# Block means of the first chunk from its own value rows, and their products apart

## The chip, the cores and the metric

The kernel runs on one core of a Trainium2 chip. The metric is the time of one execution on the device, in microseconds (us). Three runs of the kernel before took 574.43, 574.89 and 575.10 us; the median is 574.89.

## The reference

The kernel computes an attention layer and, on its output, two expert layers (MLPs).

```python
# attention: batch 2, 8 heads, 768 positions, 64 wide
k_sum = k.reshape(B, H, nb, block, D).max(axis=3)      # blocks of 32 keys
v_sum = v.reshape(B, H, nb, block, D).mean(axis=3)
scores_l = scale * q @ k^T, kept where |i - j| < 16, else -1e9
scores_s = scale * q @ k_sum^T + log(32)
a = softmax(concat([scores_l, scores_s]))              # 1e-9 added to the sum
x = a @ concat([v, v_sum])
# two expert layers, 512 -> 2048 -> 512, on 1536 tokens
h = x @ w_in;  g = relu(h) ** 2;               x = g @ w_out
h = x @ w_in2; g = 0, (h + 1) ** 2 / 4 or h;   out = g @ w_out2
```

So each query looks at a band of 16 keys to either side and at 24 block keys. Its output is a product of its probabilities with the values of the band and with the 24 block means of the values.

## The kernel before, in words

**Attention.** The queries are cut into six chunks of 256 (three in each batch), and each chunk into four pairs of heads, which makes 24 tiles. The steps of tile i have short names in a plan: S (scores: 16 matmuls, line 629), M (mask, scale and row maximum, VectorE, line 637), E (exponential, ScalarE, line 643), Q, R and N (sum, reciprocal, normalising), T (four transposes on TensorE, line 660), to (copy of the transposed probabilities out of PSUM, line 663), O (product with the values, line 671), oh and ol (the output as a high and a low part). A score tile has 96 columns for the band of 64 queries and 24 for the block keys, so the transposed probabilities have 120 rows.

The value tile of a chunk, `vwt`, holds for each of its four groups of 64 queries the 96 value rows of the band (rows 0 to 95, step vl) and under them the 24 block means (rows 96 to 119). One matmul then contracts all 120 rows. The block means are made on TensorE: step v (line 697) multiplies a tile of 128 value rows by a matrix `vx` that holds 1/32 in the place of each block, and adds up in a PSUM bank. Six such tiles of plain values (loads bl0 and bl1, line 716, into the value tile of chunk 1 and into scratch) make a batch of 24 means. Step vk copies them to `vs` in SBUF (line 706), and step vf spreads them under the value rows by a DMA from SBUF to SBUF (line 614). For chunk 0 two pairs of heads are spread by ScalarE instead (step f, line 701) and the rest by the DMA.

**Experts.** Weights come as raw 64-bit numbers (wl, line 202) and are taken apart by ScalarE, VectorE and GpSimd (dl, dq, dr, ds, dt, da, wh, wo) into a high and a low part. Step H (line 290) is the first product of an expert layer, Y (line 419) the second, with ha, hb, hh and hl between them. The first twelve such units run in between the attention tiles. Later units use products of a Strassen scheme (Pa to Pg, line 322).

**Order.** There is no scheduler. `PLAN` is a list of 2291 steps; `build` calls them one by one, and each engine runs its instructions in that order. A letter behind a number names the engine (a ScalarE, v VectorE, g GpSimd). `warm7` means seven filler matmuls into an unused bank (line 688). All loads are issued from SP in one queue, in the plan's order, and a load waits there until its buffer is free.

Of the kernel before, what the change touches and what calls it, by code (L numbers as in the profile page):

```python
# [66 lines left out]
to5a ol4 M9 wh2a wo3g O5 ha0a Q8 T6 oh5a M10 hb0 N7g H1 to6a hh0a ol5 E9 R8 wo2g km5 T7 S11 ha1a hl0g Q9 dq4 O6 vf2
N8g Y0 oh6a to7a ol6 wl6 dr4 hb1 bl2 dl4 ds4 O7 wl7 R9 dt4 T8 kl7 N9g oh7a dq5 ol7 H3 M11 wh4a da4 E10 km4 H2 dr5 hh1a
Q10 to8a hl1g S12 E11 ds5 T9 R10 M12 N10g Y1 ha2a hb2 ha3v to9a dt5 dl5 O8 wo4v wh5a S13 wl9 da5 Q11 hb3 vl4 km6 T10
dq6 wl8 H4 E12 ql4 wo5g M13 hh2a R11 oh8v H5 E13 hl2g ol8 dr6 hh3v to10a O9 N11v hl3g ha4a S14 Q13 dq7 dl6 dr7 T11 R13  # L70
ds7 hb4 H6 to11a ds6 M14 hh4a hl4g Y2 oh9v ol9 N13g ha6a km7 v6 dt6 O10 v7 ha5v wh6a da6 Q12 S15 hb6 bl3 dl7 v8 vl3
oh10v H7 E14 R12 ql5 dt7 N12v da7 hb5 Y3 ol10 wh7a M15 hh5a hl5g wo6v E15 v9 O11 v10 wo7v dq8 v11 Y4 hh6v ha7v vk5a
hl6g vk6a Q15 hb7 vk7a dr8 vk4a oh11a Y6 vf3 hh7v ds8 hl7g Q14 vf4 ua0v T12 Y7 to12a R14 dt8 N14g yo7a ol11 uf0v S16
dq9 S17 T13 M16 ug0g H8 to13a M17 dl8 E16 T14 wl10 R15 dr9 O13 N15v O12 to14a ha8v ub0v S18 oh13a E17 S19 Q16 uc0g
oh12v T15 dl9 R16 ol12 Y5 M18 to15a yo5a uh0g ol13 H9 Q17 E18 R17 M19 N16g O15 ha9a Q18 O14 E19 S20 N17g oh15v ol15
hb8 S21 Q19 T16 hh8v R19 H10 M20 hl8g to16a hb9 N19g hh9a T17 E20 M21 H11 da8 oh14v to17a ol14 ui0a S23 ha10v R18 ds9
hb10 S22 N18v E21 O17 dt9 O16 uj0v hh10a wl11 T18 da9 oh16a vl5 LW0 wh9a Y8 Q20 to18a ol16 hl9v oh17a hl10g T19 ol17
R20 Y9 M22 to19a uk0g ha11a M23 wh8a O18 E22 Q21 O19 wo9g N20v Y10 oh19a saa2g oh18a Q22 dq10 ol19 E23 wo8g T20 ol18
R21 H16 sab2v hb11 to20a N21v dq11 dr10 ul0v T21 ha16a H17 hh11a sac2v sh5a Q23 hl11g to21a sl5v hb16 dr11 um0a O21
R22 ds11 N22g O20 hh16a ud0a Y11 hl16 dt11 ha17a sad2v hb17 ds10 T22 sh4a R23 dt10 H18 hh17a sl4g wh11a hl17 oh21a  # L80
N23v dl11 dl10 H19 wl13 ue0v yo11a wl12 da10 to22v ha18v Y16 un0v da11 hb18 ha19a ol21 wh10a oh20a wo10v T23 wo11g Y17
# [733 lines left out]
```

## Time and profile before

| | |
|---|---|
| Median of three runs | 574.89 us (574.43 to 575.10) |
| The profiled execution | 576.15 us, of which the span from first to last instruction is 574.2 us |
| TensorE busy | 565.1 us, 98% of the span |
| VectorE, ScalarE, GpSimd busy | 455.6, 375.6 and 244.6 us (79%, 65%, 43%) |
| Granted TensorE clock, mean | 0.997 |
| DMA | 54.15 MB; 326, 333, 299 and 322 GB/s in the first four of 40 slices, some 75 GB/s in most of the later ones |

The page gives the busy time of each engine, the span in 40 slices, and the chain of work that ended last, followed back from the end. A second view cuts the span into stretches and gives for each the busy time of the engines, the granted clock of TensorE and the share of the DMA engines; what a stretch lacks in busy time is idle time. The timeline lists an engine's instructions in order, each with the idle time ahead of it and what ended that.

### The profile page before, as it was taken

What the parts mean: (1) busy time and instruction counts of PE and PEld (TensorE: products, weight loads), DVE (VectorE), ACT (ScalarE), POOL (GpSimd) and SP (SyncE); (2) the same over time, 40 slices, a digit from 0 to 9 for tenths busy, and PEclk for the clock granted to TensorE, in tenths of its full rate; (3) what the DMA queues carried; (4) which work ended last, traced back from release to release, by engine and by line L of the source; (5) the groups of instructions that cost most, each with busy time, mean ns of one, the idle gap of its engine ahead of it and who ended that gap; (6) DMA issues with size and microseconds to landing.
All of it is one profiled execution on the core that took longest, in us unless ns stands there. A gap on an engine that the chain in (4) does not pass through costs nothing.

```text
span 574.2 us, 11097 instructions
## 1 busy us (share of the span) xinstructions
PE 565.1 (98%) x4207; PEld 526.9 (92%) x4207; DVE 455.6 (79%) x1064; ACT 375.6 (65%) x796; POOL 244.6 (43%) x211
## 2 busy tenths in 40 slices
PE   8899999999999999999999999999999999999997
PEld 3599899999999999999999998989998988999886
DVE  5889989889987776668888988969886897756554
ACT  5789689877755554546574887867756877835450
POOL 3466576543544434535348485414443433310000
PEclk9899999999999999999999999999999999999999
DMA  8889613122222222212221102222222222000005
GB/s 326 333 299 322 209 40 94 74 73 76 74 73 74 74 74 74 75 73 75 75 84 63 42 34 74 73 74 73 75 73 72 76 73 75 1 1 0 1 0 220
DMA packets 16528, 54.15 MB, mean 94 GB/s; under 512 B 1724, under 2 KB 2332, under 8 KB 16476
## 3 DMA queue, kind: packets, MB, share of 16 engines
q1 hardware_dynamic: 16476, 53.45, 26.6%
q8 instruction: 33, 0.54, 0.4%
q14 instruction: 19, 0.16, 0.1%
HBM read 49.41 MB, written 3.15 MB: 92 GB/s over the span
## 4 chain that ended last, share of the span: by engine, by line
PE 95%; DMA 3%; ACT 1%; DVE 0%; SPq 0%; issue 0%; ACTq 0%
PE bank L419 45%; PE bank L322 36%; PE bank L290 6%; PE bank L671 2%; PE bank L629 2%; PE bank L660 2%; DMA raw<-in_wd_dram 2%; PE bank L480 1%; DMA q<-in_qd_dram 1%; PE bank L697 0%; ACT fx L213 0%; ACT s L643 0%; SPq L202 0%; ACT acc L706 0%; DVE sm L646 0%
## 5 line engine op out<-in xcount | busy, mean ns | idle before, releaser
L222 POOL TENSOR_TENSOR fr<-fx,fr 128x512 uint32<-128x512 uint32 x64 | 88.9, 1398 | 149.8 <-DVE fx L219 79.1
L386 DVE TENSOR_TENSOR gl<-bank,gh 128x384 fp32r<-128x384 f32 x120 | 65.2, 550 | 14.5 <-ACT gh L382 13.4
L322 PE MATMUL bank<-xl,wih 128*128 128x384 f32 x224 | 75.1, 335 | 0.0
L322 PE MATMUL bank<-xh,wih 128*128 128x384 f32 x224 | 74.9, 334 | 0.0
L419 PE MATMUL bank<-gh,woh 128*128 128x384 f32 (+1 forms) x272 | 64.8, 329 | 0.0
L361 ACT ACTIVATE tm<-bank,bias 128x384 f32<-128x384 f32 x62 | 35.8, 577 | 44.3 <-PE bank L322 23.9
L419 PE MATMUL bank<-gl,woh 128*128 128x384 f32 (+1 forms) x272 | 63.7, 325 | 0.0
L419 PE MATMUL bank<-gh,wol 128*128 128x384 f32 (+1 forms) x272 | 63.7, 325 | 0.0
L378 DVE SCALAR_TENSOR_TENSOR bank<-bank,tm 128x384 f32<-128x384 f32 x64 | 35.5, 561 | 29.9 <-ACT tm L374 28.8
L322 PE MATMUL bank<-xh,wil 128*128 128x384 f32 x224 | 57.0, 335 | 0.0
L322 PE MATMUL bank<-tl,wih 128*128 128x384 f32 x168 | 56.3, 335 | 0.0
L322 PE MATMUL bank<-th,wih 128*128 128x384 f32 x168 | 56.2, 334 | 0.0
L419 PE MATMUL bank<-woh,gl 128*128 128x512 f32 x180 | 55.8, 391 | 0.0
L419 PE MATMUL bank<-wol,gh 128*128 128x512 f32 x180 | 55.8, 391 | 0.0
L419 PE MATMUL bank<-woh,gh 128*128 128x512 f32 x180 | 55.7, 391 | 0.0
L448 DVE TENSOR_TENSOR acc<-bank,acc 128x384 f32<-128x384 f32 (+1 forms) x81 | 46.5, 603 | 6.1 <-PE bank L419 5.8
L213 ACT ACTIVATE fx<-raw 128x512 f32<-128x512 f32 x64 | 42.4, 669 | 8.3 <-DMA raw<-in_wd_dram 5.9
L208 ACT ACTIVATE fr<-raw 128x512 uint32<-128x512 uint32 x64 | 42.3, 671 | 8.3 <-POOL wil L258 3.0
L419 PEld LDWEIGHTS bank<-gh,woh 128*128 128x128 f32 x272 | 47.3, 188 | 0.5 <-issue 0.2
L419 PEld LDWEIGHTS bank<-gh,wol 128*128 128x128 f32 x272 | 47.5, 188 | 0.0
L419 PEld LDWEIGHTS bank<-gl,woh 128*128 128x128 f32 x272 | 47.5, 188 | 0.0
L382 ACT CAST gh<-bank 128x384 fp32r<-128x384 f32 x78 | 36.8, 479 | 15.7 <-DVE bank L378 14.4
(145 smaller groups left out, 1395.4 us busy)
## 6 DMA issues: line engine op xcount, KB each, us to landing
raw<-in_wd_dram SPq DMA_DIRECT2D x64, 512.0 KB, 3.6
vw<-in_vw_dram SPq DMA_DIRECT2D x4, 1024.0 KB, 8.1
k<-in_kd_dram SPq DMA_DIRECT2D x8, 400.0 KB, 5.9
out_dram<-acc SPq DMA_DIRECT2D x11, 256.0 KB, 3.6
q<-in_qd_dram SPq DMA_DIRECT2D x5, 512.0 KB, 8.3
vw<-in_vb_dram SPq DMA_DIRECT2D x1, 1024.0 KB, 8.9
acc<-in_vb_dram SPq DMA_DIRECT2D x2, 512.0 KB, 7.3
acc<-in_vw_dram SPq DMA_DIRECT2D x1, 1024.0 KB
```

The lines of the kernel that those rows point to most:

```text
L208: A.activation(fr[n % 2], w_raw(n, 0), AF.Copy, scale=2.0 ** -29)
L213: A.activation(f32(x), f32(hi), AF.Abs)
L222: G.tensor_tensor(fr[n % 2], fx[n % 2], fr[n % 2], ALU.add)
L290: PE.matmul(h_bank(n), a, b, start=i == 0, stop=i == len(ops) - 1)
L322: PE.matmul(q_bank(q, role), a, b, start=bool(first and i == 0), stop=i == 5, skip_group_check=not first)
L361: A.activation(a, h, AF.Relu, bias=bias[:, 1:2], scale=-1.0)
L378: V.scalar_tensor_tensor(h, h, 1.0, a, ALU.max, ALU.mult)
L382: cp(e)(hi, h if m else a)
L386: e.tensor_tensor(lo, h if m else a, f32(hi), ALU.subtract)
L419: PE.matmul(ys[j], a, b, start=f == 0 and i == 0 and (n >= 12 or j % 2 == 0), stop=f == GF - 1 and i == 2 and (n >= 12 or j % 2 == 1))
L448: V.tensor_tensor(a, y_bank(g, t, j), a, ALU.add)
L629: PE.matmul(sbank(i, 2 * h + t)[r * 64:r * 64 + 64, 0 if keys else KW:KW if keys else KN], qs[cc % 2][rows, p, j * QT:(j + 1) * QT], b, st ...
```

## The change

The block means of the first batch are made from eight tiles instead of six. Chunk 0's own value tile already holds its 256 value rows, 64 in each of its four groups, so steps v0 to v3 use that tile (96 rows) with a second matrix of weights, `vy`. It is 96 x 38 and comes from the constants by a load of its own (cl2). Steps v4 to v7 use four tiles of plain values for the other 512 rows, and the load bl1 is gone. Steps v8 to v13 make the second batch as before.

The value tile of chunk 0 no longer gets the means under its rows. The four O steps of chunk 0 multiply twice: 96 rows of probabilities with the value rows, then 24 rows with `vs` itself, added up in the same bank. Steps f and vf0 are gone. The other 20 tiles multiply as before.

The plan has 2290 steps and is in a new order up to the product `Pd2`, step 752 (the instructions around it run at about 156 us in the trace of before); from there it is the same. Of the steps that stay, 82 run on another engine: 21 from VectorE to ScalarE and 16 back, 22 from GpSimd to VectorE and 23 back. There are 36 filler matmuls for 42.

```diff
-warm11 wl0 wl1 kl0 qf0 kl1 cl0 kl2 qf1 kl3 dl0 bl0 dq0 dr0 ds0 dq1 ql1 dr1 ds1 km0 wl3 warm12 S0 dt0 bl1 dt1 da0 km1
+warm11 wl1 kl0 qf0 kl1 cl2 kl3 cl0 qf1 wl0 dl1 kl2 dq1 km0 vl0 warm4 S0 dr1 bl0 ds1 km1 S1 ql1 dt1 wl3 cl1 wh1a M1 da1
...
@@ -563,9 +563,11 @@
             V.memset(s[:, :, KN:KN + 1], 1.0e-9)
         ident = cst[:, I_OFF:I_OFF + 128]
 
+
         vx, vs, vn = acc[:, :VX_W], acc[:, 512:1024], acc[:, 4096:6144]
-        vnat = [[vwt[1][:, m] if m < 4 else acc[:, 1024 + m * 512 - 2048:1536 + m * 512 - 2048] for m in range(6)],
-                [vn[:, m % 4 * 512:m % 4 * 512 + 512] for m in range(6)]]
+        vy = acc[:KW, 64:64 + VY_W]
+        vnat = [vwt[0][:KW, j] for j in range(4)] + [vwt[1][:, m] for m in range(4)]
+        vnat += [vn[:, m % 4 * 512:m % 4 * 512 + 512] for m in range(6)]
         G.memset(vx, 0.0)
         for i in range(4):
             G.memset(vx[i * BLK:(i + 1) * BLK, NB - 4 + i:NB - 3 + i], 1.0 / BLK)
@@ -610,8 +612,7 @@
             SY.dma_start(vwt[cc][ps].rearrange("p (a j) n -> p a (j n)", a=2), vw[cc, :, ps].rearrange("a p n -> p a n"))
 
         def vs_fill(cc):
-            c = slice(0 if cc else 256, 512)
-            SY.dma_start(vwt[cc][KW:KN, :, c], vs[KW:KN, c].unsqueeze(1).to_broadcast([NB, 4, c.stop - c.start]))
+            SY.dma_start(vwt[cc][KW:KN], vs[KW:KN].unsqueeze(1).to_broadcast([NB, 4, 512]))
 
         def k_sum(n):
             V.tensor_reduce(ks[n], kp[n % NK][:, WIN:WIN + S].rearrange("p (n t) -> p n t", t=BLK),
@@ -663,13 +664,18 @@
             cp(e)(p_tile(i).rearrange("p a b -> p (a b)"), abank("t", i)[:KN])
 
         def o_mm(i):
+
             cc, p, c, n = geo(i)
-            ps = o_bank(i)
-            for j in range(4):
-                for hf in range(2):
-                    rs, r0 = slice(hf * 64, hf * 64 + 64), j % 2 * QT
-                    PE.matmul(ps[rs, j * QT:(j + 1) * QT], vwt[cc][:KN, j, p * 128 + hf * 64:p * 128 + hf * 64 + 64],
-                              p_tile(i)[:, 2 * hf + j // 2, r0:r0 + QT], start=True, stop=True)
+            ps, pr = o_bank(i), p_tile(i)
+            parts = [(vwt[cc], slice(0, KN))] if cc > 0 else [(vwt[cc], slice(0, KW)), (None, slice(KW, KN))]
+            for v, rows in parts:
+                for j in range(4):
+                    for hf in range(2):
+                        rs, r0 = slice(hf * 64, hf * 64 + 64), j % 2 * QT
+                        cs = slice(p * 128 + hf * 64, p * 128 + hf * 64 + 64)
+                        PE.matmul(ps[rs, j * QT:(j + 1) * QT], vs[rows, cs] if v is None else v[rows, j, cs],
+                                  pr[rows, 2 * hf + j // 2, r0:r0 + QT], start=cc > 0 or (v is not None and j == 0),
+                                  stop=cc > 0 or v is None, skip_group_check=cc < 1)
 
         def o_out(i):
             cc, p, c, n = geo(i)
@@ -692,28 +698,29 @@
 
         def v_sum(n):
 
-            g, m = divmod(n, 6)
+            g = n // 8
+            m = n - 8 if g else n - 2
+            w = vy[:, 6 - 2 * n:38 - 2 * n] if n < 4 else vx[:, NB - 4 - 4 * m:NB + 28 - 4 * m]
             for p in range(NP):
-                PE.matmul(v_bank(g)[p * 32:p * 32 + 32], vx[:, NB - 4 - 4 * m:NB + 28 - 4 * m],
-                          vnat[g][m][:, p * 128:(p + 1) * 128], start=m == 0, stop=m == 5)
-
-        def v_fill0(p, e):
-            cp(e)(vwt[0][KW:KN, :, p * 128:(p + 1) * 128],
-                  v_bank(0)[p * 32:p * 32 + NB].unsqueeze(1).to_broadcast([NB, 4, 128]))
+                PE.matmul(v_bank(g)[p * 32:p * 32 + 32], w, vnat[n][:, p * 128:(p + 1) * 128],
+                          start=n in (0, 8), stop=m == 5)
 
         def v_keep(n, e):
             g, p = divmod(n, NP)
             cp(e)(vs[KW:KN, p * 128:(p + 1) * 128], v_bank(g)[p * 32:p * 32 + NB])
 
         def c_load(k):
+            if k == 2:
+                SY.dma_start(vy, cd[:KW, CONST_W:])
+                return
             cs = (slice(0, M_OFF + 256), slice(M_OFF + 256, CONST_W))[k]
             SY.dma_start(cst[:, cs], cd[:, cs])
 
         def vb_load(n):
 
-            g, k = divmod(n, 2)
-            o = (vwt[1].rearrange("p m n -> p (m n)"), acc[:, 1024:2048], vn, vn[:, :1024])[n]
-            SY.dma_start(o.rearrange("p (a n) -> p a n", n=1024), vb[g, 2 * k:2 + k].rearrange("a p n -> p a n"))
+            o, g, a = {0: (vwt[1].rearrange("p m n -> p (m n)"), 0, slice(1, 3)), 2: (vn, 1, slice(0, 2)),
+                       3: (vn[:, :1024], 1, slice(2, 3))}[n]
+            SY.dma_start(o.rearrange("p (a n) -> p a n", n=1024), vb[g, a].rearrange("a p n -> p a n"))
 
         late = ExitStack()
 
...
@@ -783,7 +790,7 @@
 
 def consts():
 
-    c = np.zeros((128, CONST_W), np.float32)
+    c = np.zeros((128, CONST_W + VY_W), np.float32)
     c[:, I_OFF:I_OFF + 128] = np.eye(128, dtype=np.float32)
     qi = np.arange(QT)[:, None]
     w = np.arange(KW)[None, :]
@@ -794,6 +801,8 @@
             m = c[r * QT:(r + 1) * QT, M_OFF + i * 128:M_OFF + i * 128 + KN]
             m[:, :KW] = np.where(ok, 0.0, NEG)
             m[:, KW:] = np.log(BLK) / SCALE
+    for i in range(2):
+        c[WIN + i * BLK:WIN + (i + 1) * BLK, CONST_W + 6 + i] = 1.0 / BLK
     return c
```

On SP, the queue of the loads, the first rows before are these. `raw` is a weight tile, `k` keys, `q` queries, `cst` the mask and identity, `vw0` and `vw1` the value tiles of chunks 0 and 1, `in_vb` plain values, `acc` scratch (row lengths are of 4-byte numbers).

```order
L202 DMA raw0_74<-in_wd_dram 128x1024
L202 DMA raw1_75<-in_wd_dram 128x1024
L600 DMA k0_112<-in_kd_dram 128x800
L606 DMA q0_110<-in_qd_dram 128x512
...
L716 DMA vw1_136<-in_vb_dram 128x2x1024
L603 DMA q1_111<-in_qd_dram 128x1024
L202 DMA raw3_108<-in_wd_dram 128x1024
L716 DMA acc_73<-in_vb_dram 128x1024
L202 DMA raw2_107<-in_wd_dram 128x1024
L610 DMA vw0_135<-in_vw_dram 128x2x1024
L610 DMA vw1_136<-in_vw_dram 128x2x1024
L614 DMA vw0_135<-acc_73 24x4x256
```

And these in the change, at the same place of SP's row.

```order
L202 DMA raw1_75<-in_wd_dram 128x1024
L602 DMA k0_112<-in_kd_dram 128x800
L608 DMA q0_110<-in_qd_dram 128x512
L602 DMA k1_113<-in_kd_dram 128x800
L714 DMA acc_73<-in_cd_dram 96x38
...
L612 DMA vw0_135<-in_vw_dram 128x2x1024
L723 DMA vw1_136<-in_vb_dram 128x2x1024
L605 DMA q1_111<-in_qd_dram 128x1024
L202 DMA raw3_108<-in_wd_dram 128x1024
L717 DMA cst_109<-in_cd_dram 128x128
L202 DMA raw2_107<-in_wd_dram 128x1024
L612 DMA vw1_136<-in_vw_dram 128x2x1024
```

The own values of chunk 0 moved from the place behind all plain values to the place ahead of them; one weight tile moved behind the first keys and queries; four tiles of plain values come in one load.

On TensorE, before, the four products of chunk 0 stand together, with a transpose behind them (`pt` and, for the fourth, `acc` hold the transposed probabilities).

```order
L629 MATMUL bank1_64<-ks2_122,q1_111 64x24 x2
L671 MATMUL bank6_69<-pt0_132,vw0_135 64x64 x8
L671 MATMUL bank1_64<-pt1_133,vw0_135 64x64 x8
L671 MATMUL bank2_65<-pt2_134,vw0_135 64x64 x8
L671 MATMUL bank3_66<-acc_73,vw0_135 64x64 x8
L660 MATMUL bank7_70<-cst_109,s0_128 120x128 x4
```

In the change, the first product of chunk 0 on TensorE and what stands around it.

```order
L630 MATMUL bank3_66<-ks3_123,q1_111 64x24 x2
L676 MATMUL bank6_69<-pt0_132,vw0_135 64x64 x8
L676 MATMUL bank6_69<-pt0_132,acc_73 64x64 x8
L661 MATMUL bank7_70<-cst_109,s2_130 120x128 x4
L630 MATMUL bank5_68<-k2_114,q1_111 64x96 x2
```

Each product became two rows of eight matmuls into one bank, the second on the block means in `acc`; the first one moved ahead of a transpose and a score tile.

## Rows read from the trace of the kernel before

**Rows 1.** The page: busy time of the engines; the chain by line.
```profile
PE 565.1 (98%) x4207; PEld 526.9 (92%) x4207; DVE 455.6 (79%) x1064; ACT 375.6 (65%) x796; POOL 244.6 (43%) x211
...
PE bank L419 45%; PE bank L322 36%; PE bank L290 6%; PE bank L671 2%; PE bank L629 2%; PE bank L660 2%; DMA raw<-in_wd_dram 2%; PE bank L480 1%; DMA q<-in_qd_dram 1%; PE bank L697 0%; ACT fx L213 0%; ACT s L643 0%; SPq L202 0%; ACT acc L706 0%; DVE sm L646 0%
```

**Rows 2.** Stretches: us, length, busy time by engine, clock, DMA share, GB/s.
```profile
0.00:8.15 8.15, 6.87 (x23) 2.61 (x23) 2.54 (x13) 3.19 (x4) 0.72 (x9) 1.00 0.75 260
8.15:18.95 10.80, 9.47 (x213) 5.92 (x212) 10.29 (x52) 5.36 (x15) 7.24 (x6) 1.00 1.03 413
18.95:25.20 6.25, 3.57 (x62) 2.02 (x60) 4.78 (x18) 6.13 (x17) 1.99 (x3) 1.00 0.85 335
25.20:28.90 3.70, 3.68 (x80) 3.31 (x82) 3.03 (x15) 2.75 (x7) 1.61 (x2) 0.54 0.73 221
28.90:34.45 5.55, 5.46 (x178) 4.83 (x176) 4.77 (x23) 5.18 (x16) 2.68 (x3) 1.00 0.96 309
34.45:156.00 121.55, 121.55 (x1451) 116.99 (x1448) 111.15 (x321) 99.52 (x244) 70.13 (x60) 1.00 0.40 135
```

**Rows 3.** Timeline of TensorE: start, length, what, count, idle before and releaser.
```profile
1.28 6.94 PE L688 MATMUL bank<-acc 128*128 128x512 bf16 x23 [1.28 <-DVE s L563]
...
15.52 0.65 PE L697 MATMUL bank<-vw,acc 128*32 128x128 f32 x16
16.09 0.40 PE L629 MATMUL bank<-k,q 64*64 64x96 f32 x8
...
20.22 0.43 PE L697 MATMUL bank<-acc 128*32 128x128 f32 x8 [1.16 <-DMA acc<-in_vb_dram]
...
25.22 0.88 PE L660 MATMUL bank<-cst,s 128*120 128x128 f32 x4 [1.26 <-ACT pt L663]
...
32.55 0.62 PE L660 MATMUL bank<-cst,s 128*120 128x128 f32 x4
33.15 0.40 PE L629 MATMUL bank<-k,q 64*64 64x96 f32 x8
...
33.84 0.69 PE L671 MATMUL bank<-acc,vw 120*64 120x64 f32 x16
34.45 0.39 PE L290 MATMUL bank<-xh,wih 128*128 128x256 f32 x1
```

**Rows 4.** Line 716, plain value loads, up to 40 us: duration, starts, landing.
```profile
L716 SPq DMA_DIRECT2D vw<-in_vb_dram x1: 387/387/387, 5.9 to 5.9; - x1
L716 SPq DMA_DIRECT2D acc<-in_vb_dram x1: 328/328/328, 9.0 to 9.0; - x1
...
DMA to landing us min/median/max: 8.9/10.0/11.2
```

**Rows 5.** Timeline of ScalarE.
```profile
18.98 0.66 ACT L213 ACTIVATE fx<-raw 128x512 f32<-128x512 f32 x1 [3.40 <-DMA raw<-in_wd_dram]
...
26.24 1.17 ACT L701 COPY vw<-bank 24x512 f32<-24x512 f32 x2
...
33.66 1.26 ACT L643 ACTIVATE s<-s,sm 128x120 f32<-128x120 f32 x4
34.82 0.37 ACT L680 CAST xh<-bank 128x256 fp32r<-128x256 f32 x1
35.07 0.59 ACT L663 COPY acc<-bank 120x512 f32<-120x512 f32 x1
```

**Rows 6.** Timeline of SP, issues of loads.
```profile
9.58 0.33 SPq L202 DMA_DIRECT2D raw<-in_wd_dram  x1
10.61 8.87 SPq L610 DMA_DIRECT2D vw<-in_vw_dram  x2
```

**Rows 7.** Line 202, weight loads, up to 40 us: time to landing.
```profile
DMA to landing us min/median/max: 4.7/4.9/11.9
```

**Rows 8.** Timeline of VectorE.
```profile
32.60 0.28 DVE L637 CUSTOM_DVE_ANT_0 s<-bank,cst 128x120 f32<-128x120 f32 x1
...
33.42 0.65 DVE L646 TENSOR_REDUCE sm<-s 128x4 f32<-128x484 f32 x1
```

More of the change, by code (lines that the diff above doesn't have):

```diff
@@ L46 @@
 VX_W = NB + 28
+VY_W = 38
 def bits(u):
@@ L67 @@
[L67 to L81, printed above, removed]
@@ new lines @@
+ha11a M22 hl10g O18 Y9 N20g oh18a E22 ol18 ol17 wo9g M23 O19 ul0g T20 Q22 oh19a wh8a ol19 H17 Q21 dq10 saa2g to20a
+dr10 E23 sab2g R21 H16 dr11 hb11 R22 wo8v sh5a ds10 sac2g Q23 O20 ha16a sl5v Y10 sad2g hh11a um0a ha17v hl11v N21g
+hb16 R23 ds11 sh4a Y11 hh16a N23g oh20a hl16 hb17 T21 dl11 dt11 H18 hh17a to21a N22v wl13 da11 hl17 ol20 T22 un0v H19
+to22a wh11a dt10 uo0g ha18a yo11v hb18 O21 ha19a O22 wo11v T23 oh22a oh21a Y16 ua1g hh18a ol22 ud0a ol21 sl4v ub1g
+hb19 hl18 wh10a Y17 ue0v dl10 uc1g to23a wl12 up0v hh19a O23 da10 LS0 ud1a oh23v dq13 ol23 H20 hl19 uq0a ue1g dr13
@@ new lines @@
+hh41a dr25 hb43 ds24 dl24 ds25 dt24 Y39 hh43a dt25 wh24a da24 hl42 wl27 hl41 wl26 ya12 Pa5 da25 hl43 Pc5 Ca5a wo24g
+Pb5 Cc5a wh25a wo25v dq27 Pd5 Vb5 saa6v Pa6 dr27 sab6g ya15 ya13 Pf5 sh13a ya14 dq26 sl13v Pe5 ha44a ha45v hb44 Y40
+hh44a hb45 hl44 dr26 sac6v Vc5 dl27 sad6g Y41 ha46v hh45a ds26 sh12v ds27 hl45 Pg5 dt27 Ca6v wl29 da27 Y42 ha47a hb47
+hb46 sl12g hh47v wh27a hh46v Pd6 hl47 hl46 dt26 Y43 ha48a dl26 ya16 dq29 wl28 da26 hb48 ya18 Pc6 ya17 hh48a wo27g
+wh26a ya19 Pb6 hl48 Cc6a dr29 wo26g Y44 Vb6 ds29 dt29 Y45 Pf6 Pe6 ha49a dl28 Y46 hb49 dq28 hh49a dr28 dl29 Vc6 ds28
@@ new lines @@
+Y116 hb121 hb122 hc121 hc122 wh62a hh121v Y117 ha123a wo62g hl121 hh122v hb123 da63 ya90 Y118 Ca25v hl122 hc123 Pd25
+Pc25 ha124a Pb25 Cc25a hb124 Y119 hh123a hc124 Vb25 hh124v hl123 ya92 Pf25 hl124 ya93 Pe25 ha125a Pa26 Vc25 hb125
+ha126a hc125 Pg25 wh63v wo63v hb126 Y120 ha127a hc126 hh125a hh126a hl125 Y121 hb127 hl126 Ca26a hc127 hh127a Pc26
+Pb26 Cc26v hl127 Pd26 Vb26 ya94 Pf26 ha128a Pe26 ha129a Pa27 hb129 hb128 Y122 hc128 hh128v Y123 ya96 ya97 Y124 hl128
+Vc26 hc129 ha130a hh129v Y125 ya98 hb130 hc130 hl129 hh130a Pg26 hl130 Ca27v Pc27 ha131v Pb27 Pd27 Cc27v hb131 Vb27
@@ L162 @@
+Y126 ha132a hb132 hc132 Y127 hc131 ya100 hh132v Pe27 hl132 ya101 Pf27 Vc27 hh131v ha134a Pg27 hl131 ha133a Y128 hb134
+hb133 hc134 hc133 hh134a Y129 ha135a hb135 Y130 hc135 hh135a hh133a hl135 ya102 Y131 ya104 hl134 yd104 yd97 ya106 yd96
+hl133 Z1 yd101 ya105 yd100 yd106 yd98 Z3 Z0 za3 za1 zd3 yd105 zd1 yd102 Z2 za0 zd0 za2 zd2
 """
@@ L740, in build @@
                 "E": s_exp, "Q": s_sum, "R": s_inv, "N": s_norm, "T": t_mm, "to": t_out, "O": o_mm, "oh": o_hi, "ol": o_lo,
-                "v": v_sum, "f": v_fill0, "vk": v_keep, "dl": w_low,
+                "v": v_sum, "vk": v_keep, "dl": w_low,
                 "da": w_add, "wh": w_hi, "wo": w_lo, "H": h_mm, "ha": h_act, "hb": h_sq, "hc": h_mul, "hh": h_hi, "hl": h_lo,
```

164 lines of the change are left out of this document (80 added, 84 removed).

## The prediction

> **What bounds the kernel now.** I read the page first: TensorE is busy for 565.1 of 574.2 us and stands on nearly the whole chain of waits [rows 1]. Such a kernel gets shorter only where TensorE stands still, fills its time with filler matmuls, runs at the lower clock, or gets less to do. The view by stretches shows where that is [rows 2]. From 34.45 us on, TensorE works without a gap to 156 us, at full clock. Before 34.45 us it is idle for 1.28, 1.33, 2.68, 0.02 and 0.09 us (each stretch less its busy time), and nearly all of this lies before 25.2 us. The timeline of TensorE then says what fills the rest [rows 3]. The first 23 filler matmuls run from 1.28 us for 6.94 us, and the first score tile comes behind them. At 20.22 us a block sum has waited 1.16 us for the value tiles of line 716, and at 25.22 us a transpose 1.26 us for a copy out of PSUM. In the stretch that follows the granted clock is 0.54 on average, so part of it ran at 1.2 GHz: 3.68 us of work took what 0.54 x 3.68 = 1.99 us takes at 2.4 GHz, a loss of 1.69 us. Four products of probabilities and values (line 671) lie in it.
>
> What TensorE waits for is the loads. The DMA engines are full (share 1.03, 413 GB/s) up to 18.95 us and nearly so to 25 us [rows 2]. The first value load of line 716 is issued at 5.9 us and lands 8.9 us later, at 14.8; the second is issued at 9.0 and lands 11.2 us later, at 20.2 [rows 4]. So what counts in the first 25 us is the order of the bytes in the one queue, and after that the plain sum of TensorE's work. The first point at which TensorE never waits again is the first expert matmul (H0, line 290), which starts at 34.45 us [rows 3]. I ask how much earlier H0 starts after the change.
>
> **Where the bytes stand.** I count KB ahead of and including a load, from the shapes in the two orders, and give each load the landing time of the load of before at the same place in the queue. Before: up to the first value load, 2 x 512 (weights) + 4 x 400 (keys) + 2 x 256 (queries) + 192 + 1024 = 4352 KB, landed 14.8. The queries and a weight tile after it end at 5376 KB; ScalarE waits for that weight tile until 18.98 us [rows 5]. The second value load ends at 5888 KB (20.2 us), the next weight tile at 6400 KB: issued at 9.58 us, landed 11.9 us later, the longest of line 202, at 21.5 [rows 6, 7].
> After: the chunk's own values end at 4366 KB, so they land at 14.8. The four plain tiles end at 5390 KB: 18.95. The second queries end at 5902 KB: 20.2. Weight tile 3 ends at 6414 KB: 21.5. The rate alone would give the plain tiles an earlier time: 1038 KB more than the 4352 at 413 GB/s is 2.6 us, or 17.4 us. The trace shows the later time at this place, and I take it, since it is a row; 17.4 is the other end.
>
> **The change part by part.**
> *Start.* One 512 KB weight tile goes behind the first keys and queries, worth 1.3 us at 413 GB/s, and 15 fillers stand ahead of the first score tile for 23. It can start some 1.3 us sooner. This gains nothing by itself, since the plain tiles at 18.95 still hold the block sums; it only moves the two first softmax tiles ahead of them. 20 more fillers (5 and 15) cover the wait for keys, one the wait for values; they are 36 in all for 42, and none stands on the path.
> *Block sums.* Fourteen steps for twelve; eight for six in the first batch. One costs 0.29 us (two take 0.57 us, from 15.52 to 16.09) [rows 3]. The four on own values run before 18.95, in time that TensorE has; four are left.
> *Removed.* Two copies into the value tile (line 701, 1.17 us of ScalarE) [rows 5], a DMA from SBUF to SBUF and 512 KB of loads.
> *Products multiplied apart.* The four products of chunk 0 get 8 more matmuls each, on 24 rows. The trace of before has no matmul of that shape. Lower end: nothing, if they run beside the 96-row ones. Next row: a whole product of 8 matmuls, 0.61 us (33.84 to 34.45 us) [rows 3]. A gain is excluded, since nothing is taken from the first half. I take 0.61, because the columns that are streamed are as many; 4 x 0.61 = 2.44 us more work for TensorE. The upper end, 0.61 and two drains of the array, is a rival below.
> *New waits.* The second half of a product waits for the copy of its block means (line 710), which in ScalarE's row stands behind an exponential for pairs 0 and 1. Behind it on TensorE wait a transpose, a score tile and the next products. The own value load of chunk 1 waits on SP until the last block sum of the first batch (about 20.7 us by the sum below), with the next queries and keys behind it; before, the same two loads of line 610 held SP from 10.61 to 19.48 us [rows 6]. That is 1.2 us later, for tiles whose first reader stands over 9 us behind, so I cost it at nothing; if that cover is gone, it is at most the 1.2 us.
>
> **The sum.** After 18.95 us TensorE has up to H0: 4 block sums x 0.29 = 1.16; 5 transposes x 0.60 (32.55 to 33.15 us) = 3.00; 7 score tiles x 0.69 (33.15 to 33.84) = 4.83; 4 products x 1.22 = 4.88; one product of the next chunk, 0.61 [rows 3]. Together 14.48 us, so H0 starts at 33.43 us instead of 34.45: 1.02 us earlier. This holds only if TensorE does not wait in between. ScalarE: after weight tile 3 (21.5 us) it has four exponentials at 1.16 us (33.66 to 34.82), three PSUM copies of at most 0.59, the last of which frees the fifth transpose's bank, and seven smaller steps of 0.25 to 0.65, 2.9 us in all by my count: done at about 30.8; the sum wants it at 31.5. VectorE, once score tile 5 is there (about 21.4 us), has five mask-and-maximum steps of 0.82 us (32.60 to 33.42), four sums of at most 0.65, and eleven small steps, an estimate of 4 us for them, until it has read score tile 8, whose bank tile 10 takes: done at about 32.1; the sum wants it at 32.7 [rows 5, 8]. Each keeps some 0.6 us. TensorE also has less idle time in this stretch than it had, so I leave the clock at full.
> After H0 TensorE does the same work as before. Up to 156 us the order of the steps is new, with 21 steps from VectorE to ScalarE, 16 back, 22 from GpSimd to VectorE, 23 back, so the loads stay level (VectorE is busy 111 of 122 us there [rows 2]); from there the order is the old one, step by step. So 1.0 us stays to the end. In the profile's own time: span 574.2 - 1.0 = 573.2, and 576.15 - 1.0 = 575.15 with what lies around the span. The median of the runs shown, 574.89, is 1.26 below that execution; the forecast on it is 573.9 us.
>
> **The rivals.**
> *The plain tiles land at 17.4.* For it: the rate of 413 GB/s in the same stretch. Against it: at this place in the queue the weight tile came at 18.95. The last block sums then end at about 19.5, when the second queries let the next score tile start; from there 12.7 us remain (the sum less four block sums and the transpose among them): H0 at 32.2, 2.2 us earlier, if ScalarE and VectorE follow: 572.7 us.
> *The clock falls in the new stretch.* TensorE now stands idle from about 17.5 to 18.95 and then works without a break; a fall to 1.2 GHz anywhere from there to H0 costs what it cost before, 1.69 us, in a stretch that has no other wait to hide it: 0.7 us slower, 575.6. For it: the granted clock fell after the 1.26 us gap at 25.22. Against it: after the gap up to 20.22 us it did not [rows 2, 3].
> *The split products drain the array: slower.* Each of the four products now changes from 96 rows to 24 and back, eight changes. If TensorE finished all it had before each, a change would cost the tail of a step: at least the 0.08 us by which a product's row reaches into the next step (33.84 + 0.69 against 34.45), at most, an estimate, a whole step of block sums, 0.29 us [rows 3]. Eight of these give 2.3 us: 1.3 us slower, 576.2. It decides from 0.13 us for each change on. Against it: the score tile on 64 rows at 33.15 and the product on 120 rows behind it follow each other without a gap.
> The Trainium skill (TensorEngine Tiling (Array Packing), Key Properties) says that changing the tiling mode drains TensorE; by it this rival is the forecast, and the trace, with a tail of 0.08 us at most at such a change, bears out a small one only.
> *The new order waits later on.* VectorE has 10 us to spare in 122; one late step in each of a few places takes the gain back: 574.9.
>
> **How the numbers follow.** Forecast 0.40; early landing 0.23; clock 0.15; drain 0.10; later waits 0.12. A measurement of this kernel tells about 0.2%, 1.15 us, from no change. The forecast's 1.0 us lies just inside; half of its chance goes to faster. Faster: 0.20 + 0.23 + 0.01 = 0.44. Within: 0.20 + most of the clock's and the later waits' shares, 0.19 = 0.39. Slower: 0.10 and the rest of those two, 0.07 = 0.17. The range, 572.4 to 575.8, reaches from a little under the early landing to the clock's case, and leaves out the drain. The forecast's own range is 573.3 to 574.5: a tail of 0.08 us at each of the eight changes makes it 0.6 us later, and second halves that are half hidden make it 1.2 us sooner, of which ScalarE and VectorE allow about half.
>
> **What would show it.** Right: the block sums of the plain tiles start at about 19 us, a product of chunk 0 takes 1.2 us, TensorE has no wait from there on, the granted clock is 1.00 from 19 to 33 us, and H0 starts at about 33.4. Wrong: plain tiles at 17.4 and H0 near 32; a stretch at 1.2 GHz; products over 1.4 us; or H0 on time and waits of TensorE for ScalarE or VectorE between 34 and 156 us.

## The result, and the profile after

The kernel after takes 579.5 us (median of 5 runs, 579.15 to 580.28), the kernel before 574.89 (574.43 to 575.1 in as many): a ratio of 1.0083, 95% interval 1.0068 to 1.0098. It is slower by 4.6 us. The forecast was 573.9 us, its range 572.4 to 575.8. The profiled execution of after took 579.16 us with a span of 577.3.

The view by stretches of the kernel after, cut where the granted clock changes (columns as in [rows 2]):

```profile
0.00:8.15 8.15, 5.78 (x47) 2.45 (x47) 2.15 (x11) 2.52 (x3) 0.72 (x9) 1.00 0.75 249
8.15:18.95 10.80, 8.81 (x159) 5.49 (x163) 10.29 (x46) 7.47 (x21) 4.94 (x5) 1.00 1.03 413
18.95:25.20 6.25, 6.25 (x196) 5.34 (x196) 4.73 (x31) 5.02 (x14) 4.41 (x4) 1.00 0.90 313
25.20:28.49 3.29, 3.04 (x84) 2.52 (x76) 2.77 (x15) 3.24 (x11) 1.26 (x2) 1.00 0.78 270
28.49:35.31 6.82, 6.57 (x106) 5.60 (x108) 3.75 (x16) 3.66 (x10) 2.17 (x3) 0.50 0.96 351
35.31:157.90 122.59, 122.31 (x1484) 116.80 (x1481) 108.32 (x316) 99.35 (x246) 72.53 (x60) 1.00 0.37 124
```

From 18.95 to 25.20 us TensorE is busy all the time, where it was busy 3.57 of 6.25 us before [rows 2]. But from 28.49 to 35.31 us it runs at 1.2 GHz: 6.82 us for the work of 3.41. The same view of the kernel before, cut at its own change of clock:

```profile
25.45:28.86 3.41, 3.41 (x78) 3.02 (x78) 2.77 (x14) 2.50 (x6) 1.57 (x2) 0.50 0.77 233
```

The timeline of TensorE in the kernel after (start, length, what, count, idle before and its releaser) answers to [rows 3]:

```profile
1.28 5.03 PE L694 MATMUL bank<-acc 128*128 128x512 bf16 x15 [1.28 <-DVE s L563]
7.33 0.40 PE L630 MATMUL bank<-k,q 64*64 64x96 f32 x8 [1.02 <-DMA q<-in_qd_dram]
...
16.95 1.08 PE L705 MATMUL bank<-vw,acc 96*32 96x128 f32 x32
18.50 0.42 PE L705 MATMUL bank<-vw,acc 128*32 128x128 f32 x8 [0.47 <-DMA vw<-in_vb_dram]
...
22.77 0.69 PE L676 MATMUL bank<-pt,vw 96*64 96x64 f32 x16
23.38 0.68 PE L676 MATMUL bank<-pt,acc 24*64 24x64 f32 x16
23.99 0.66 PE L661 MATMUL bank<-cst,s 128*120 128x128 f32 x4
...
27.88 0.45 PE L676 MATMUL bank<-acc,vw 96*64 96x64 f32 x8
28.74 0.70 PE L676 MATMUL bank<-acc,vw 96*64 96x64 f32 x8 [0.42 <-issue]
29.37 1.12 PE L676 MATMUL bank<-acc 24*64 24x64 f32 x16
30.42 1.11 PE L661 MATMUL bank<-cst,s 128*120 128x128 f32 x4
...
36.30 0.38 PE L290 MATMUL bank<-xh,wih 128*128 128x256 f32 x1
...
94.09 0.74 PE L419 MATMUL bank<-gl,woh 128*128 128x256 f32 x4 [0.20 <-POOL s L656]
```

The plain tiles come at 18.50 us. A product of the first chunk takes 1.22 us (22.77 to 23.99), its second half 0.61. A second half (29.37) and a transpose (30.42) within the low clock take 1.1 us where they took 0.68 and 0.66 (lengths of rows overlap a little). H0 starts at 36.30 us; the forecast had it at 33.43, the trace of before at 34.45 [rows 3]. From H0 to the end of the span there are 577.3 - 36.30 = 541.0 us; before there were 574.2 - 34.45 = 539.75 [rows 3]. So the profile shows 1.85 us lost by H0 and 1.25 behind it.

### The profile page after: what moved, and what is told of

The parts are those of the page before. It is cut to its first block, busy times and chain, and to the rows that moved or that the text cites. A ratio compares the mean times of both kernels' runs of the same rounds, so it can differ in the third digit from the quotient of the medians.

```text
span 577.3 us, 11228 instructions
## 1 busy us (share of the span) xinstructions
PE 568.6 (98%) x4278; PEld 530.7 (92%) x4281; DVE 452.1 (78%) x1059; ACT 375.6 (65%) x798; POOL 247.4 (43%) x212
## 4 chain that ended last, share of the span: by engine, by line
PE 91%; DVE 3%; ACT 2%; POOL 1%; DMA 1%; issue 1%; SPq 0%; POOLq 0%; DVEq 0%
PE bank L419 44%; PE bank L322 35%; PE bank L290 5%; PE bank L676 2%; PE bank L630 2%; PE bank L661 2%; PE bank L480 1%; DMA k<-in_kd_dram 1%; DVE s L638 1%; ACT s L644 1%; DVE ks L618 0%; DVE sm L647 0%; POOL xl L540 0%; POOL s L656 0%; PE bank L705 0%
## 5 line engine op out<-in xcount | busy, mean ns | idle before, releaser
L222 POOL TENSOR_TENSOR fr<-fx,fr 128x512 uint32<-128x512 uint32 x64 | 87.4, 1376 | 146.1 <-DVE fx L219 80.4
```

Of the source, the lines that this page charges most:

```text
L222: G.tensor_tensor(fr[n % 2], fx[n % 2], fr[n % 2], ALU.add)
```

## The experiments

Theory A: the stretch at 1.2 GHz is the loss, and the trace of before, which had a shorter one, was not typical. Theory B: the split products alone are the loss. Theory C: the new order of the steps behind H0 loses the rest. In each result "clock" is the mean granted clock of a whole execution: 3.4 us at half clock, in which 1.7 us are lost, take off 0.003.

**1. The kernel before once more, nothing edited.**

> The kernel before once more, unchanged, to see how it runs in executions other than the one whose trace the forecast was made from; that one took 576.15 us, 1.26 more than the median of 574.89. Theory A (the clock): the stretch at 1.2 GHz from 25.45 to 28.86 us was not there, or was shorter, in the faster executions. Then a new trace shows the granted clock at 1.00 throughout 25 to 34 us, the first expert matmul (H0) at about 32.7 us instead of 34.45, and spans near 573.0 us. Rival: every execution has that stretch, H0 stands at 34.4 in each, and the 1.26 us lie somewhere else; then span and clock read 573 us and 0.997 with the stretch still there.

Measured: 574.96 us, ratio 1.0002 (0.9993 to 1.001), clock 0.997 in one of 11 executions and 0.999 or 1.0 in ten. Its trace, by stretches, and, from the timeline, the first chunk's products, a stop in a score tile, and the first row of H0:

```profile
25.20:28.90 3.70, 3.70 (x132) 3.38 (x131) 3.40 (x20) 3.63 (x11) 1.93 (x2) 1.00 0.75 231
28.90:34.45 5.55, 4.77 (x126) 4.12 (x127) 4.57 (x19) 5.08 (x15) 3.17 (x3) 1.00 0.97 328
```

```profile
26.66 1.74 PE L671 MATMUL bank<-pt,vw 120*64 120x64 f32 x48
28.23 0.64 PE L671 MATMUL bank<-acc,vw 120*64 120x64 f32 x16
28.80 0.65 PE L660 MATMUL bank<-cst,s 128*120 128x128 f32 x4
...
31.13 0.24 PE L629 MATMUL bank<-ks,q 64*64 64x24 f32 x2 [0.72 <-issue]
...
33.66 0.39 PE L290 MATMUL bank<-xh,wih 128*128 128x256 f32 x1
```

The clock stays at 2.4 GHz, H0 starts at 33.66 us, 0.8 sooner than in the trace that the forecast used, and 573.4 - 33.66 = 539.7 us follow. Of 85 executions of the kernel before beside the experiments (this one's among them) 21 have a clock under 0.9985. It costs little there: of the 74 that served for comparison, those took 575.0 us in the median, the others 574.8. The two traces suggest why: at full clock TensorE idles 0.78 us between 28.90 and 34.45, and 0.09 behind the low clock [rows 2]. But 0.72 of the 0.78 is one stop in the midst of a score tile, for which the view names no releaser ("issue"), and two traces do not show that waits take up the fall in the other executions.

**2. Eight fillers between the first chunk's products.**

```
- ... S7 vk0a E5 N2g M4 O0 M7 ... vk1a O1 to2a ... E7 O2 dt3 ... N4g O3
+ ... S7 vk0a E5 N2g M4 warm2 O0 M7 ... vk1a warm2 O1 to2a ... E7 warm2 O2 dt3 ... N4g warm2 O3
```

> The kernel after with two filler matmuls ahead of each of the four products of the first chunk, eight in all, 1.7 us of work at full clock (0.213 us each). Theory A: the stretch at 1.2 GHz (28.49 to 35.31 us, where 6.83 us do the work of 3.41) is what TensorE got for a long run of small fp32 matmuls, and fillers between them prevent it: 579.5 - 3.4 + 1.7 = 577.8 us, H0 at about 34.6 us, granted clock 1.00. Theory B (the products multiplied apart simply cost more work and the clock fell for another reason): the fall stays, and the fillers are added, at full or half clock: 581.2 to 582.9 us.

Measured: 579.6 us, ratio 1.0094 (1.0073 to 1.0114), but clock 0.997 in one execution only and 0.999 or 1.0 in five. Its trace, by stretches, shows full clock where the kernel after had half:

```profile
25.20:28.90 3.70, 3.54 (x85) 2.52 (x84) 2.90 (x15) 2.92 (x10) 1.50 (x2) 1.00 0.82 268
28.90:34.45 5.55, 5.39 (x144) 4.44 (x145) 3.58 (x15) 4.38 (x12) 1.74 (x2) 1.00 0.96 350
```

The fillers hold the clock and H0 comes at 35.78 us instead of 36.30, but the time is the same. What used up the 3.4 us is in the timeline: the fillers' 1.7 us, 0.16 us of idle time in front of three of the four pairs, plain tiles 0.2 us later, and two stops in the midst of a step, one before H0 and one behind it, where 541.8 us follow (0.8 more than in the kernel after):

```profile
35.16 0.24 PE L631 MATMUL bank<-k,q 64*64 64x96 f32 x1 [0.44 <-issue]
...
93.66 0.34 PE L677 MATMUL bank<-pt,vw 120*64 120x64 f32 x4 [0.79 <-issue]
```

Theory A held for the clock, not for the time.

**3. Without the second halves.**

```
- parts = [(vwt[cc], slice(0, KN))] if cc > 0 else [(vwt[cc], slice(0, KW)), (None, slice(KW, KN))]
+ parts = [(vwt[cc], slice(0, KN if cc > 0 else KW))]
```

> The kernel after without the second halves of the first chunk's products: the block means' share of that chunk's output is left out, so 32 matmuls on 24 rows are gone and nothing stands in their place. At full clock they cost 4 x 0.61 = 2.44 us. If the 24-row matmuls are what brought the clock down, the fall goes too: 579.5 - 2.4 - 3.4 = 573.7 us and H0 at 30.5 us. If the clock falls for the whole run of small matmuls, whatever their rows, the fall stays, earlier or later: 579.5 - 2.4 (up to 3.5, where two of the halves ran at 1.2 GHz) = 576.0 to 577.1 us. If the halves ran beside other work, almost nothing: 579 us or more.

Measured: 576.51 us, ratio 1.0036 (1.0021 to 1.0051); clock 0.991 to 0.997 in 7 of 11 executions. So the clock falls without the halves too. The four at full clock took 575.1 to 576.5 us: even 2.44 us less work does not make the new start faster than the kernel before. In its trace, at full clock, H0 starts at 32.73, not at 30.5: TensorE waits for ScalarE's copy ahead of a product and for GpSimd ahead of a transpose.

```profile
PE bank L676 <- ACT pt L664: 1.3, 1, 1.3
...
PE bank L661 <- POOL s L656: 0.5, 1, 0.5
```

(Waits of TensorE: line waited with, releaser, us in total, times, longest.)

**4. The old order behind the new start.**

```
  wl0 ... (as after) ... ol3 H0
- km5 oh4a vf2 E8 da3 ol4 wl7 R7 M9 O5 wl6 ha0a wh3a T6 ...
+ da3 wh3a E8 R7 oh4a ol4 M9 wo3g O5 ha0a Q8 T6 oh5a M10 ...
```

> The kernel after up to its first expert matmul (H0), and behind it all steps that are left in the order of the kernel before, on the engines that they had there. Theory C: the new order of the steps behind H0 costs the 1.25 us by which the distance of the two traces grows from 1.85 us at H0 to 3.1 us at 165 us (two waits of 0.36 and 0.25 us and about 0.6 us in the neighbourhood of small matmuls): 578.2 us. Theory A alone: the later order is worth nothing, and the whole difference stands before H0: 579.5 us. Worse than 579.5: the old order does not fit the state that the new first part leaves.

Measured: 579.28 us, ratio 1.0079 (1.0067 to 1.0091), clock 0.991 to 0.994 in all five. Behind H0 the trace has 577.5 - 37.3 = 540.2 us, 0.8 fewer than after, but its plain tiles came later (TensorE waited 1.50 us for them, 0.47 in the trace of after), and H0 with them. The time does not bear theory C out.

**5. The new order behind the old start.** The mirror of the edit above: the kernel before up to H0, then the kernel after.

> The kernel before up to its first expert matmul (H0), and behind it all steps that are left in the order of the kernel after, on the engines that they have there. The first part of the kernel before rarely has a stretch at 1.2 GHz, so the order behind H0 is seen alone. Theory C: that order is worse by the 1.25 us that the two traces show between H0 and 165 us: 574.85 + 1.25 = 576.1 us. Rival: it is worth nothing, and the 1.25 us came from the state in which the new first part leaves the engines: 574.85 us.

Measured: 577.22 us, ratio 1.0045 (1.0031 to 1.0059); clock under 0.9985 in 3 of 6 executions, and the three at full clock took 576.9 to 577.7 us. H0 starts at 33.08 us; 542.1 us follow, 2.3 more than with the old order. Half of that is one wait right behind H0, in the timeline of TensorE:

```profile
35.94 0.69 PE L670 MATMUL bank<-acc,vw 120*64 120x64 f32 x16 [1.15 <-DVE xl L683]
```

A product waits until VectorE has read out the product before it. So the new order is no better than the old, but much of its price here is at the seam; what it costs in its own kernel this run does not say exactly.

**6. Second halves of two matmuls instead of eight.**

```
+ for hf in range(2):
+     PE.matmul(ps[hf * 64:hf * 64 + 64], vs[KW:KN, ...], pr[KW:KN, 2 * hf:2 * hf + 2],
+               start=False, stop=True, ...)
```

> The kernel after with the second half of each of the first chunk's products as 2 matmuls of 24 rows and 256 columns instead of 8 of 64 columns; the same numbers are computed. If the columns streamed set the price, a half costs what 4 transposes of 128 columns cost, 0.60 us for 0.61, and nothing changes but for the clock: 579.5 us. If each matmul has a price of its own, 24 of the 32 are saved: up to 4 x 0.4 = 1.6 us, 577.9 us. Theory A says that in both cases the stretch at 1.2 GHz stays, with a granted clock near 0.994 over the whole execution, and that the time stays above 577.

Measured: 576.65 us, ratio 1.0033 (1.002 to 1.0046). The clock is under 0.9985 in 4 of 11 executions, where the kernel after has it in 5 of 5. The timeline of TensorE, at full clock throughout:

```profile
27.41 0.65 PE L679 MATMUL bank<-pt,acc 24*64 24x256 f32 x4
27.98 0.69 PE L674 MATMUL bank<-acc,vw 96*64 96x64 f32 x16
28.60 0.65 PE L679 MATMUL bank<-acc 24*64 24x256 f32 x4
29.18 0.65 PE L661 MATMUL bank<-cst,s 128*120 128x128 f32 x4
...
32.90 0.39 PE L290 MATMUL bank<-xh,wih 128*128 128x256 f32 x1
```

A wide half takes 0.58 us (28.60 to 29.18), the eight narrow ones 0.61: the streamed columns set nearly all of the price, not the number of matmuls. So this is the work of the kernel after with its clock kept, and H0 starts at 32.90 us. The seven executions at full clock took 575.4 to 577.2 us; their median, 576.1, is still more than that of the kernel before. The expectation "above 577" was wrong: the stretch at 1.2 GHz came less often. The clock is not the whole difference, though: two executions of this run with a mean clock like that of the kernel after (0.993 and 0.994) took 578.1 and 577.7 us, where the kernel after took 579.2 to 580.3. Where their low clock lay no trace shows.

**7. The split alone, in the kernel before.** Its products (line 671) become those of after; the steps f0a, f1a and vf0 go.

> The kernel before, its order kept, with one part of the change alone: the first chunk's products multiplied apart, 96 rows and 24 rows, and so without the two copies into the value tile and the small transfer behind them. 4 x 0.61 = 2.44 us are added on TensorE. Theory B (the split alone makes the loss): 574.85 + 2.44 = 577.3 us, and with a stretch at 1.2 GHz, which the 24-row matmuls would bring, 579 to 580.7 us. Theory A with room: TensorE idles about 2.8 us between 20 and 32 us in a trace of the kernel before at full clock, 1.06 of it for a copy that stands behind ScalarE's two fills; a good part of the halves fits there, the clock stays, and the time is 575 to 576 us.

Measured: 579.05 us, ratio 1.0075 (1.0055 to 1.0096); clock under 0.9985 in 3 of 6 executions. The three at full clock took 578.0 to 578.2 us. In the trace of one of them the four products stand behind each other, and H0 at 36.05 us, 2.4 us later than in run 1:

```profile
26.49 0.69 PE L674 MATMUL bank<-pt,vw 96*64 96x64 f32 x16
27.11 0.68 PE L674 MATMUL bank<-pt,acc 24*64 24x64 f32 x16
27.72 0.69 PE L674 MATMUL bank<-pt,vw 96*64 96x64 f32 x16
...
31.39 0.65 PE L659 MATMUL bank<-cst,s 128*120 128x128 f32 x4
...
36.05 0.39 PE L289 MATMUL bank<-xh,wih 128*128 128x256 f32 x1
```

Four products take 4.90 us here (26.49 to 31.39), 1.22 each. In run 1 the four unsplit ones stand behind each other too and take 2.14 us (26.66 to 28.80), about 0.53 each and not 0.61: a product costs 0.61 us only between steps of another shape. So the split adds 2.76 us on TensorE, more than the 2.44 expected; run 10 shows that the changes of shape are part of it. Theory B has its price in the old order, where the wait for ScalarE's copy (1.07 us) stayed and hid none of it.

**8. The eight fillers ahead of transpose 3.**

```
- ... E3 warm15 T1 ... v4 Q0 E2 T3 R0
+ ... E3 warm15 T1 ... v4 Q0 E2 warm8 T3 R0
```

> The kernel after with eight filler matmuls ahead of transpose 3 (at 18.86 us), before the first products instead of between them; the same 1.7 us of work as the eight fillers that were put ahead of the products, with which the clock stayed at 1.00. If the chip goes by what TensorE does in the stretch of the products, the fall stays, a little later: clock 0.994, 579.5 + 1.7 = 581.2 us. If what counts is the whole run of small matmuls from 12.5 us on, fillers anywhere in it do: clock 0.999 or more, and 579.6 us as with the other eight.

Measured: 581.64 us, ratio 1.0116 (1.0099 to 1.0134), clock 0.994 to 0.997 in all five. Against run 2, with the fillers between the products: the same work, and the clock falls in all five executions, where it fell in one of six. So fillers some 4 us ahead of the products do not do what fillers between them do. That what TensorE does among the products decides is not shown by this: in the trace the products run at full clock (24.25 to 31.66 us), with a wait of 1.17 us for VectorE ahead of the fourth, and the low clock comes behind them, from 32.60 to 36.02 us.

**9. Wide halves and the old order behind H0**, the edits of 6 and 4 together.

> The kernel after with second halves of 2 matmuls of 256 columns and, behind its first expert matmul, the steps that are left in the order of the kernel before. The span less the time of H0 was 539.7 to 540.2 us in four traces with the old order behind H0 and 540.6 to 542.1 in six with the new one, a difference of 1.5 us between the means. If this adds to what the wide halves gave (576.65): 575.1 us in the median, 574.6 where the clock stays at full, no slower and no faster than the kernel before. If the old order does not fit the new first part, as in the run of the kernel after with it (579.28 for 579.5): 576.4 us.

Measured: 576.03 us, ratio 1.002 (1.001 to 1.003). H0 at 32.73 us, but 540.6 us behind it: the sixth product waits 0.71 us for VectorE at 35.13, the wait that run 5 showed. Executions at full clock took 575.0 to 576.1.

**10. Second halves on 120 rows.**

```
- [(vwt[cc], slice(0, KW)), (None, slice(KW, KN))]
+ [(vwt[cc], slice(0, KW)), (None, slice(0, KN))]      # and G.memset(vs[:KW], 0.0) at the start
```

> The kernel after with the second halves on all 120 rows instead of 24: the block means' tile has zeros in its upper 96 rows, so the same is computed, with the same count of matmuls and columns; GpSimd writes the zeros once at the start. If the clock falls because the 24-row matmuls keep few rows of the array at work, it stays at full in most executions (0.997 or more) and the time is that of the kernel after without its 1.2 GHz stretch, 576 to 577 us. If rows at work have nothing to do with it: granted clock 0.994 again and 579.5 us.

Measured: 581.1 us, ratio 1.0111 (1.0097 to 1.0125), clock 0.994 to 0.997 in all four. For the clock it is inconclusive. In the trace the products run at full clock, and the low clock comes behind them; but TensorE also waits 1.13 and 2.94 us for nothing that the profile shows, in the midst of a product and of a score tile, and these set the time:

```profile
29.63 0.45 PE L677 MATMUL bank<-acc,vw 96*64 96x64 f32 x8 [1.13 <-issue]
...
36.92 0.20 PE L631 MATMUL bank<-ks,q 64*64 64x24 f32 x1 [2.94 <-issue]
```

For the price of the split the run tells more. Ahead of the first stop, at full clock, these halves stand behind each other:

```profile
27.11 0.69 PE L677 MATMUL bank<-pt,vw 96*64 96x64 f32 x16
27.63 0.64 PE L677 MATMUL bank<-pt,acc 120*64 120x64 f32 x16
28.09 0.40 PE L677 MATMUL bank<-acc,vw 96*64 96x64 f32 x8
```

A product of 96 and 120 rows takes 0.98 us (27.11 to 28.09), one of 96 and 24 rows in run 7 1.23 (26.49 to 27.72, the start of its second product). Matmuls and columns are the same in number; only the rows differ. So a change between 96 and 24 rows costs about 0.12 us that a change between 96 and 120 does not, 1.0 us for the eight changes.

**11. The block sums alone, in the kernel before.** Own values go ahead of the plain tiles, eight block sums for six, weight tile 3's steps later, tile filled.

> The other part of the change alone, in the order of the kernel before: block means from the chunk's own value rows and four plain tiles loaded for six, while the value tile is filled as before and one product does the whole. Own values go ahead of the plain tiles, and the steps of weight tile 3, which now lands about 2.5 us later, stand further back. No matmul is added but eight of block sums, in time that TensorE has. The wait for the plain tiles (0.6 to 1.2 us in traces of the kernel before) should go: if nothing takes its place, 574.9 - 0.8 = 574.1 us. If TensorE then only waits longer for ScalarE's copy behind it (1.06 to 1.26 us at the next transpose), nothing is gained: 574.9 us. If the later weight tile holds ScalarE: 575.5 us or more.

Measured: 579.53 us, ratio 1.0076 (1.0063 to 1.0089), clock 0.993 to 0.997 in all five, with no second halves in it. A failed experiment for the time: the second queries now stand behind 1 MB of plain tiles, and the old order wants them ahead of the block sums:

```profile
19.70 0.60 PE L632 MATMUL bank<-k,q 64*64 64x96 f32 x8 [2.83 <-DMA q<-in_qd_dram]
```

For the time it shows only that the new order of loads does not fit the old order of the early steps.

**12. New start, old order behind it, tile filled.**

```
- ... S7 vk0a E5 N2g M4 O0 M7 dq2 wo0g T2 E4 Q5 S6 ds3 dr2 vk1a O1 to2a Q4 vf1
+ ... vf0 ... S7 f0a E5 N2g M4 O0 M7 f1a dq2 wo0g T2 E4 Q5 S6 ds3 dr2 O1 vk0a to2a vk1a Q4 vf1
```

> The kernel after with the old order behind H0 (579.28 us, span 577.5 with H0 at 37.3) and now without the split: the first chunk's value tile is filled again, by two copies of 0.59 us on ScalarE and a small transfer, and one product on 120 rows does the whole. 32 matmuls, 2.44 us of TensorE's work, go. Theory D (the 24-row halves bring the 1.2 GHz stretch): the clock stays in most executions, H0 at about 32.7 us, as in the run without the block means, and with 539.8 to 540.6 us behind it and 1.9 around the span 574.6 to 575.2 us: no slower than the kernel before. Rival: any long run of small matmuls does it; then the clock falls in most executions, for one stretch (0.997, a loss of up to 1.7 us), and the time is 576 us; if ScalarE's two more copies or the small transfer behind the loads hold the products, 576 us or more at full clock.

Measured: 577.13 us, ratio 1.0047 (1.0033 to 1.0061): 2.15 us less than run 4, which has the split in place of the fills and some copies in another order. Clock under 0.9985 in 4 of 6, so theory D is not borne out: the clock falls without the halves. (Of the kernel before, 6 of 11 executions measured with this run had a fall, and 3 of 22 of those measured with runs 1 to 4.) Without the halves TensorE waits for ScalarE, which now has the fills:

```profile
27.53 1.08 PE L674 MATMUL bank<-pt,vw 120*64 120x64 f32 x16 [2.06 <-ACT pt L666]
```

**13 and 14. The same with less waits, and with four fillers in the wait.** ScalarE's copy to2a goes ahead of E4 and the weight step, H1 ahead of O5; run 14 has warm4 ahead of O2 besides.

> The last kernel (new start, filled tile, old order behind H0: 577.13 us) with two waits of its trace taken away by order alone: ScalarE's copy for product 2 goes ahead of two exponentials and a weight step (TensorE waited 2.06 us for it), and the second expert matmul goes ahead of the sixth product (0.87 us for VectorE). If both waits go and nothing takes their place: about 576.7 in its full-clock executions - 1.5 - 0.8 = 574.4 us, faster than the kernel before by 0.4. If the exponential moved back holds a later transpose instead: 575.5 us. If the clock falls for the long run of small matmuls without a wait: granted clock 0.997 in most executions and up to 1.7 us more.

> The same as the kernel with less waits, with four filler matmuls (0.85 us) ahead of the third product, where TensorE waited. If they stand in a wait they cost nothing, or 0.85 us if the wait is gone: 574.4 to 575.3 us at full clock. If fillers between the products hold the clock, as eight of them did in the kernel after, it is 0.999 or more in nearly all executions; if not, it falls as often as in the kernel without them.

Measured: 579.04 us, ratio 1.0075 (1.0061 to 1.0088), and 578.55, ratio 1.006 (1.0046 to 1.0074). Both expectations failed: the wait went on to the next transpose, which waits for GpSimd's normalising step, itself held by VectorE (run 13):

```profile
30.32 0.65 PE L663 MATMUL bank<-cst,s 128*120 128x128 f32 x4 [3.41 <-POOL s L658]
```

ScalarE is busy without a pause from 21.3 us to past 29 there; moving its steps here only moved the wait. The clock fell in 5 of 5 and in 4 of 5. Four fillers ahead of that wait do not hold it. No kernel of this study beats the kernel before.

## Why the prediction was wrong

**The places of the bytes and the block sums: right.** Plain tiles 18.50 us (18.95 foretold), weight tile 3 in use from 21.13 (21.5), four block sums left. The first score tile came 0.8 us sooner (1.3 foretold).

**The sum to H0: right at full clock.** H0 at 33.43 was forecast. In the trace of after 3.41 us of the 36.30 are lost to the clock, which leaves 32.89; in run 6, nearly the same work at full clock, H0 is at 32.90. The 0.5 us between are the plain tiles: from their first block sum to H0 run 6 took 14.38 us, the sum says 14.48.

**The step that failed is "I leave the clock at full".** The term for the clock was put at nothing because TensorE has less idle time in the stretch. It has: from 18.50 us on there is no wait over 0.1 us until the one of 0.42 us that ends at 28.74. The clock fell within that one all the same, in this trace, and it fell in all five executions of after: 6.82 us at 1.2 GHz, 3.41 lost. So less idle time was no reason to put the term at nothing. The rival of the clock had the right mechanism, but a price from the trace of before, one stretch of 3.41 us and 1.69 lost. Behind the new start the loss also stays: in run 9 the four executions at 0.997 took 1.4 us more in the median than the seven at full clock, while in the kernel before a fall costs 0.15 us in the median. Why it costs so little there is open.

**The reference point was not typical.** The prediction took the 1.26 us between the profiled execution and the median as an amount to subtract from both kernels, and counted its gain from that execution's H0 at 34.45. Run 1 has H0 at 33.66. So 0.8 of the 1.02 us gained were gained against a low clock that most executions of before don't have. The rest is in doubt too: run 1 has its stop of 0.72 us ahead of H0 and run 6 has none, so without it the old start would have H0 at 32.94, the new one at 32.90.

**"So 1.0 us stays to the end" failed too.** Against run 1 (span 573.4) the trace of after is 3.9 us longer: 3.41 of clock, -0.77 for the rest of the start (33.66 to 32.89), and 1.26 behind H0 (541.00 less 539.74). With profiled executions 0.4 above and 0.3 below their medians this is the 4.6 us. The 1.26 is where the rival of later waits (574.9) looked, though its price was too low: one wait is the row at 94.09 us. Run 5 shows that the new order is the worse one behind the old start, run 4 that the old one brings the time little behind the new start. How the 1.26 us divide among waits and the neighbourhood of small matmuls stays open.

**The drain of split products: there, and already in the price.** The forecast set the drain aside, and its price held: 1.22 us for a product, no more. But the 0.61 us of a half came from a product between steps of another shape, so it has a change of shape in it; in a row of products of one shape a product takes 0.53 us (run 1). Run 10 against run 7 gives the change its price, about 0.12 us where 96 rows meet 24, so the added work is 2.76 us, not 2.44. The sum to H0 did not need that difference. The Trainium skill (TensorEngine Tiling (Array Packing), Key Properties) says that a change of tiling mode drains TensorE; these traces agree, with about 0.12 us for each change.

**What stays open is what brings the clock down.** Fillers between the products hold it (fallen in 1 of 6), the same fillers earlier don't (5 of 5). Narrow second halves in this start, with no fillers among them, go with a fall in 10 of 10 executions (the kernel after, run 4), wide ones of nearly the same length in 8 of 22 (runs 6 and 9), none at all in 7 of 11, a filled tile in 13 of 16 (12 to 14) and, in the old order, in 5 of 5 (run 11); narrow halves in the old order in 3 of 6 (run 7). Rows at work could not be told apart, since run 10 was upset by other waits. So second halves are not needed for a fall, and that narrow ones make it certain or longer is not shown: the shares come from groups of executions in which the kernel before itself fell in 3 of 22 to 6 of 11. In the traces of after and of run 4 the fall comes within the stop in the midst of the fourth product, in run 10 within its stop of 2.94 us; stops in runs 1 and 6 (0.72 and 0.66 us) passed at full clock. Whether a stop has to do with the fall was not tried.

## What to carry to other kernels

Before a gain is counted from a profiled execution, compare its granted clock, and its stops without a releaser, with those of other executions: a low stretch in it is a gain that most of them already have. A tight run of small matmuls needs a price at half clock for its whole length; here that was 3.41 us, more than the whole forecast gain. Splitting a matmul by rows costs the streamed columns twice, whatever the rows, and a change of shape besides where the parts differ as 96 and 24 rows do here. A price read from one row holds for the neighbours that this row had.
